# Linear attention and a Fourier feed-forward layer on one core: query loads split by row class and ordered by need, reciprocal roots taken per class, early k/v loads in another ring, and the first part of the program held in the planner's order

## Chip, cores, metric

One NeuronCore of a Trainium2 chip runs the whole program. The metric is the device time of one execution in microseconds; for the kernel before it is the median of three executions. The profile is one further, profiled execution.

## What is computed

For each of 8 batches, with 8 heads, 576 tokens and 64 channels per head:

```python
kv  = einsum('bhsd,bhse->bhde', k, v)
out = einsum('bhsd,bhde->bhse', q, kv)
x   = out / sqrt(mean(out * out, -1) + 1e-6) * g_norm      # then [batch, 576, 512]
X   = real(fft(fft(x, axis=1), axis=2))
u   = x + X
un  = (u - mean(u)) / sqrt(var(u) + 1e-6)
y   = u + maximum(un @ w_ch1, 0) @ w_ch2                   # 512 -> 2048 -> 512
```

Everything is float32; the weights come in as 64-bit floats.

## The kernel before

The work has two phases. Phase 1 goes batch by batch through attention, normalisation and the Fourier transform, and fills TensorE's gaps with a part of the feed-forward layer. Phase 2 is the rest of the feed-forward layer, block by block of 512 tokens.

One batch in phase 1 runs through these steps, in the names of the code:

- `plan_kv`: SyncE's queue loads k and v in four pairs of heads (`km`, `vm`, 256 KB each, from a ring `kv` of six buffers, L460) and a remainder (`kr`, `vr`, L469). For batch 0 the v loads go through ScalarE's queue. TensorE multiplies them into `ps_k` (L481).
- `plan_q_load` and `plan_q`: the queries come in two loads of 576 KB, one for each half of the tokens (`side`), at L504, and one more row of 2 KB (L510). The tokens of a half are dealt to three classes `j` (every third token). TensorE transposes each class (`ps_q`, L529), ScalarE copies it to `fq` (L533).
- `plan_out`: one output class `t` needs one query class of each side. TensorE writes two banks `ps_o` (L554); ScalarE copies (L569) and squares (L574) them, VectorE sums the squares (L578), GpSimd multiplies by `g_norm` (L589).
- `plan_y`: the reciprocal roots of all three classes at once: square root on ScalarE (L607), reciprocal on VectorE (L614), one refinement on GpSimd (L610, L618 to L620), the product on VectorE (L623).
- `plan_fold`: VectorE multiplies by the root (L651) and folds the halves (`ab`, L662), GpSimd adds and subtracts (`xe`, L669), ScalarE rounds to the high part `xh` (L675), GpSimd leaves the low part `xl` (L678).
- `plan_seq` (L693, L706, L710) and `plan_chn` (L727, L739, L747, L757): the Fourier transform along tokens and channels as matmuls with cosine and sine tables `cs` and `cd`, loaded and split once by `plan_dft` (L428, L431, L434).
- `plan_turn`: the result is transposed (L813) into blocks `unTh`, `unTl` of 512 tokens (L822, L825).

`plan_w` turns the feed-forward weights from 64-bit floats into two float32 parts: load (`raw`, 512 KB, L282), an Abs step on ScalarE (L285), five steps on VectorE (L292 to L302), a sum (L857), for the first matrix a mean (L307, L315) and its subtraction (L319), and the split (L861, L866). `plan_early` runs three of the sixteen slices of the feed-forward layer for a block (`ps_h` L354, `hh` L364, `hl` L367, `acc` L372) as soon as its tokens and the weights are there.

The order comes from a planner. Every step is an `op` with an engine, a cost in nanoseconds, a rank, the steps it follows and the ring buffers it takes; `Plan.run` walks through time, and on every free engine emits the ready step of lowest rank whose buffers are free. The ranks are 10 x batch + stage, and 1000 and more for the feed-forward filling. What it emits is then ordered once more by the Tile framework's scheduler, which may move an instruction past another on its engine. The rings are a fixed count of buffers per kind (`RINGS`); among them `h` has six buffers, used by `hh` and `hl`, and `part` two, used by the feed-forward partial sums.

## Time and profile before

| | us |
|---|---|
| median of 3 executions | 1024.72 |
| lowest, highest | 1024.54, 1029.22 |
| profiled execution | 1026.22 |
| its span | 1024.4 |
| TensorE busy | 993.9 (97%) |
| VectorE, ScalarE, GpSimd busy | 472.0, 322.4, 320.6 |

A view by windows gives, for each stretch of the span, the busy time and the number of instructions of TensorE, its weight loads (PEld), VectorE (DVE), ScalarE (ACT) and GpSimd (POOL), then TensorE's granted clock as a share of full speed, the mean busy share of the 16 DMA engines, and GB/s. Asked for one engine, it gives that engine's alone. In a timeline a row has its start, its length, engine, line, operation, output and inputs, and in brackets the idle time before it with what ended it; SPq is SyncE's queue issuing transfers, and the length of such a row is how long the queue was held. In the list of waits a row has who waited, for whom, total microseconds, times, and the longest. The chain of waits has start, length and what.

### The profile page before, as it was taken

The page shows a single profiled execution, that of the slowest core. Times are in us where ns is not written, and L with a number is a line of the kernel's source. Part 1 is how long each engine was busy: PE and PEld are TensorE (multiplying, and loading weights), DVE is VectorE, ACT ScalarE, POOL GpSimd, SP SyncE. Part 2 cuts the span into 40 slices and gives each one's busy share as a digit, 9 for nine tenths or more (in the row PEclk, how much of TensorE's full clock was granted, in tenths as well). Part 3 has the DMA queues.
Part 4 walks back from the last instruction along what each step waited for, and adds up shares of the span by engine and source line. Part 5 has one row for each costly group of instructions (what it writes and reads, how often), then busy time and mean ns, then how long its engine had stood idle before and what let it go on. Part 6 is the DMA issues. An engine that isn't in the chain of part 4 may idle for free.

```text
span 1024.4 us, 15026 instructions
## 1 busy us (share of the span) xinstructions
PE 993.9 (97%) x5866; PEld 839.4 (82%) x5866; DVE 472.0 (46%) x838; ACT 322.4 (31%) x655; POOL 320.6 (31%) x332
## 2 busy tenths in 40 slices
PE   4698999999999999999999999999999999999998
PEld 4697898889888888888888888888888888888886
DVE  4758775654588689998131314131221311311211
ACT  2456565555545434334221212021121021210110
POOL 0555876864865131225722303020020010110000
PEclk9998999999999999999999999999999999999999
DMA  9979979663246766645552515140320400400101
GB/s 245 253 164 280 190 214 263 168 182 139 88 162 212 275 206 253 228 136 175 155 177 74 182 51 170 71 139 1 125 81 0 165 21 1 164 1 1 42 1 41
DMA packets 109194, 140.70 MB, mean 137 GB/s; under 512 B 51790, under 2 KB 76418, under 8 KB 104516
## 3 DMA queue, kind: packets, MB, share of 16 engines
q1 hardware_dynamic: 105588, 132.28, 42.4%
q0 software_dynamic: 1920, 6.29, 2.0%
q10 hardware_dynamic: 1616, 1.18, 0.4%
q8 instruction: 46, 0.75, 0.3%
q14 instruction: 24, 0.20, 0.1%
HBM read 88.33 MB, written 51.40 MB: 136 GB/s over the span
## 4 chain that ended last, share of the span: by engine, by line
PE 93%; DMA 2%; DVE 2%; SPq 1%; issue 1%; ACT 0%; POOL 0%; DVEq 0%; ACTq 0%; POOLq 0%
PE ps_h L354 38%; PE acc L372 38%; PE ps_o L554 4%; PE ps_f L727 3%; PE ps_f L693 3%; PE ps_k L481 3%; PE ps_q L529 2%; PE ps_t L813 2%; DMA vm<-in_v_dram 2%; DVE x L651 1%; DMA qt<-in_q_dram 1%; SPq L510 1%; PE ps_w L315 0%; SPq L460 0%; DVE unTl L825 0%
## 5 line engine op out<-in xcount | busy, mean ns | idle before, releaser
L354 PE MATMUL ps_h<-unTh,w 128*128 128x512 f32 x1152 | 357.1, 391 | 0.0
L372 PE MATMUL acc<-w,hh 128*128 128x512 f32 x1152 | 345.0, 391 | 0.2 <-DVE unTl L825 0.2
L367 DVE SCALAR_TENSOR_TENSOR hl<-ps_h,hh 128x512 fp32r<-128x512 f32 x144 | 99.2, 689 | 379.8 <-ACT hh L364 377.5
L354 PEld LDWEIGHTS ps_h<-unTh,w 128*128 128x128 f32 x1152 | 215.4, 188 | 44.0
L372 PEld LDWEIGHTS acc<-w,hh 128*128 128x128 f32 x1152 | 214.9, 188 | 44.3 <-issue 0.3
L364 ACT ACTIVATE hh<-ps_h 128x512 fp32r<-128x512 f32 x144 | 85.9, 597 | 472.1 <-PE ps_h L354 442.9
L354 PE MATMUL ps_h<-unTl,w 128*128 128x512 f32 x576 | 224.5, 390 | 0.0
L372 PE MATMUL acc<-w,hl 128*128 128x512 f32 x576 | 213.1, 390 | 0.0
L354 PEld LDWEIGHTS ps_h<-unTl,w 128*128 128x128 f32 x576 | 108.3, 188 | 22.7
L372 PEld LDWEIGHTS acc<-w,hl 128*128 128x128 f32 x576 | 107.9, 188 | 22.5
L1133 POOL DMA_INDIRECT uu<-u_scr,rowidx x24 | 23.4, 974 | 286.2 <-DVE uu L1186 175.6
L589 POOL TENSOR_TENSOR x<-x,gb 96x512 f32<-96x512 f32 (+1 forms) x48 | 61.9, 1308 | 55.2 <-ACT x L569 40.6
L1152 POOL TENSOR_TENSOR uu<-uu,up 128x512 f32<-128x512 f32 x36 | 45.7, 1293 | 44.5 <-ACT up L1149 44.5
L554 PEld LDWEIGHTS ps_o<-kvt,fq 64*96 64x96 f32 (+1 forms) x768 | 42.7, 185 | 5.6 <-issue 3.2
L554 PE MATMUL ps_o<-kvt,fq 64*96 64x64 f32 (+1 forms) x768 | 47.0, 274 | 0.3 <-ACT fq L533 0.3
L481 PE MATMUL ps_k<-vm,km 128*64 128x64 f32 x512 | 28.7, 261 | 17.6 <-DMA vm<-in_v_dram 16.7
L1096 POOL TENSOR_TENSOR w<-wap,w 128x512 fp32r<-128x512 f32 x18 | 23.3, 1295 | 70.1 <-ACT w L1095 70.1
L1186 DVE SCALAR_TENSOR_TENSOR uu<-acc,rs_yb,uu 128x512 f32<-128x512 f32 x36 | 25.2, 745 | 42.5 <-PE acc L372 42.5
L578 DVE TENSOR_REDUCE ss<-ps_o 96x8 f32<-96x512 f32 (+1 forms) x48 | 32.2, 682 | 26.2 <-ACT ps_o L574 26.0
L669 POOL TENSOR_TENSOR xe<-ab 96x256 f32<-96x256 f32 (+1 forms) x48 | 37.5, 803 | 19.8 <-DVE ab L662 19.7
L693 PE MATMUL ps_f<-cs,xh 96*128 96x290 f32 (+1 forms) x192 | 41.8, 312 | 0.4 <-DVE x L651 0.4
L481 PEld LDWEIGHTS ps_k<-vm,km 128*64 128x64 f32 x512 | 22.9, 166 | 22.4 <-DMA km<-in_k_dram 16.2
(103 smaller groups left out, 1009.1 us busy)
## 6 DMA issues: line engine op xcount, KB each, us to landing
raw<-in_moe_w_ch_dram SPq DMA_DIRECT2D x32, 512.0 KB, 7.6
qt<-in_q_dram SPq DMA_DIRECT2D x16, 576.0 KB, 9.2
unT_scr<-unTh SPq DMA_DIRECT2D x9, 1024.0 KB
unT_scr<-unTl SPq DMA_DIRECT2D x9, 1024.0 KB, 6.3
part_scr<-part SPq DMA_DIRECT2D x36, 256.0 KB, 4.1
unTh<-unT_scr SPq DMA_DIRECT2D x9, 1024.0 KB, 4.9
unTl<-unT_scr SPq DMA_DIRECT2D x9, 1024.0 KB, 7.0
up<-part_scr SPq DMA_DIRECT2D x36, 256.0 KB, 3.0
```

Source lines behind the costliest of these rows:

```text
L354: nc.tensor.matmul(ps, w[c][:, kc * P : (kc + 1) * P], unT[a][:, kc, :], start=(idx == 0), stop=(idx == 3 * KC - 1),)
L364: nc.scalar.activation(hh, ps, AF.Relu)
L367: nc.vector.scalar_tensor_tensor(hl, ps, 0.0, hh.bitcast(F32), ALU.max, ALU.subtract)
L372: nc.tensor.matmul(acc, hpair[a][:, i * P : (i + 1) * P], w[c], start=(first and n == 0), stop=(last and n == 2),)
L481: nc.tensor.matmul(ps.t[s * D : (s + 1) * D, pr * D : (pr + 1) * D], km[:, s, j, :] if j < 4 else kr[:, h, :], vm[:, s, j, :] if j < 4 els ...
L554: nc.tensor.matmul(pss[s].t[:n, at : at + D], fqs[side].t[half, m, :n], kvt.t[half, m], start=True, stop=True,)
L578: nc.vector.tensor_reduce(ss.t[0][:n, :, t, s::2], pss[s].t[:n].rearrange("p (u m e) -> p u m e", u=2, e=D), AX.X, ALU.add,)
L589: nc.gpsimd.tensor_tensor(v_, v_, gb[:n].unsqueeze(1).to_broadcast([n, H, D]), ALU.mult)
L669: nc.gpsimd.tensor_tensor(o[:, s], a[:, 0], a[:, 1], ALU.subtract if s else ALU.add)
L693: nc.tensor.matmul(ps.t[:, :NS], xs[t].t[a][:n, part, ch * P : (ch + 1) * P], cs[:n, part, c, t, :], start=(idx == 0), stop=(idx == 8),)
L727: nc.tensor.matmul(ps.t[:n, :ND], pt.t[a][:, part, ch, offs[t] : offs[t] + n], cd[:, part, c, ch, :], start=(idx == 0), stop=(idx == 5),)
L1152: nc.gpsimd.tensor_tensor(us[j][i], us[j][i], part, ALU.add)
```

## The change

It has six parts.

- **Queries of batch 0 by class.** Each side's load becomes three loads of one class each (240 in the planner's size instead of 720), ranked by output class: side 0's class j by j/4, side 1's by (2-j)/4. A transpose follows its own class's load only.
- **Roots of batch 0 by class.** `plan_y` is called once per output class and works on a third of the columns; the temporaries `rs_s` and `rs_y` move into the ring `two`. The fold of a class follows its own root.
- **Rings.** The last pair of k and v of batch 0 and the last two of batch 1 take buffers of ring `h`; `ab` and `xe` of batch 0's third class take the two of ring `part`.
- **Weights.** The early weights' ranks become 4, 5, 6 (they were 4, 5, 6 as `rank(0, FOLD) + f` too), their loads' ranks 2, 4, 11 instead of 0, 3, 11.
- **Costs in the planner.** A pair of k and v counts 1080 instead of 520, an output class 1540 instead of 900, the copies of `plan_turn` more per column; TensorE's steps count twice until three steps of `plan_seq` have run.
- **The pin.** Each instruction that the planner emits up to 75,000 ns of its own time gets an order edge, without a semaphore, to the one emitted before it on its engine, so that the framework's scheduler keeps the planner's order there, on all five engines.

```diff
+EARLY_KV = (1, 2)
+W_CONV = (4, 5, 6)
+W_RANK = (2, 4, 11)
+PIN_UNTIL = 75000
...
+    def pin(self, emit, now):
+        tc = self.tc
+        traced = tc.nc.cur_bb.bb.instructions
+        start = len(traced)
+        emit()
+        traced = tc.nc.cur_bb.bb.instructions
+        for i in traced[start:]:
+            if i.engine not in self.pinned or now > PIN_UNTIL:
+                continue
+            last = self.last.get(i.engine)
+            if last:
+                tc.add_manual_dep(
+                    i, last,
+                    mybir.DependencyInfo(
+                        mybir.DependencyClass.NoSync, mybir.DependencyReason.DATA
+                    ),
+                    reason="the plan's order",
+                )
+            self.last[i.engine] = i.name
...
-                    o.emit()
-                    self.trace.append((t, t + o.cost, eng, o))
-                    end = free[eng] = t + o.cost
+                    self.pin(o.emit, t)
+                    cost = o.cost * (2 if eng == "PE" and cold > 0 else 1)
+                    cold -= o.dense
+                    self.trace.append((t, t + cost, eng, o))
+                    end = free[eng] = t + cost
...
-                main = Buf("kv", lambda c=c: qkv.tile([P, 2, 4, D], F32, name=c + "m", tag="m", bufs=RINGS["kv"]))
+                if b < 2 and pr >= NPAIR - EARLY_KV[b]:
+                    main = Buf("h", lambda c=c: base.tile(
+                        [P, 2, 4, D], F32, name=c + "m", tag="r", bufs=RINGS["h"]
+                    ))
+                else:
+                    main = Buf("kv", lambda c=c: qkv.tile(
+                        [P, 2, 4, D], F32, name=c + "m", tag="m", bufs=RINGS["kv"]
+                    ))
...
-            mm.append(op("PE", 520, rank(b, KV), go, ld + lds, [ps, kvt] + ts + rest))
+            mm.append(op("PE", 1080, rank(b, KV), go, ld + lds, [ps, kvt] + ts + rest))
...
+        if b == 0:
+            ld = [[dma(
+                240, rank(b, QT) + (2 - j if side else j) / 4,
+                lambda j=j: nc.sync.dma_start(
+                    qt.t[:TR, j].rearrange("p (h d) -> p h d", h=H), src[:, j]
+                ),
+                bufs=[qt],
+            )] for j in range(3)]
...
-        a = op("PE", 900, r, mm, done, [kvt, x, ss] + pss + fqs)
+        a = op("PE", 1540, r, mm, done, [kvt, x, ss] + pss + fqs)
...
+        n = TR + 1 if t is None else rows[t]
+        ts = slice(None) if t is None else slice(t, t + 1)
+        def of(a):
+            return a[:n].rearrange("p (s t h) -> p s t h", s=2, t=3)[:, :, ts]
...
-        ab, xe = e2_buf("ab"), e2_buf("xe")
+        if b == 0 and t == 2:
+            ab, xe = (Buf("part", part_tile) for _ in range(2))
+        else:
+            ab, xe = e2_buf("ab"), e2_buf("xe")
...
+        yp = bank_buf("ps_y")
+        if b == 0:
+            ys = [plan_y(b, ss, reds[t] + [one_row], yp, t) for t in range(3)]
+        else:
+            ys = [plan_y(b, ss, sum(reds, []), yp)] * 3
...
-                    plan_w(which, f, lambda: wA, rank(0, FOLD) + f, [], (0, 3, 11)[f])
+                    plan_w(which, f, lambda: wA, W_CONV[f], [], W_RANK[f])
```

The order of the instructions changes on every engine. Three places on two of them follow; the line numbers of the changed kernel are its own, some 40 to 60 higher.

On SyncE, at the start of the program, after the first k pair and its remainder, these transfers stand before (`raw` is a feed-forward weight, `gb` is `g_norm`, `qt` a query load):

```order
L460 DMA km<-in_k_dram 128x2x256 x2
L282 DMA raw<-in_moe_w_ch_dram 128x4x256
L460 DMA km<-in_k_dram 128x2x256
L282 DMA raw<-in_moe_w_ch_dram 128x1024
L412 DMA gb<-in_g_norm_dram 128x64
L504 DMA qt<-in_q_dram 96x24x64
L510 DMA qt<-in_q_dram 1x8x64
L504 DMA qt<-in_q_dram 96x24x64
```

And at the same place now:

```order
L507 DMA km<-in_k_dram 128x2x256 x3
L452 DMA gb<-in_g_norm_dram 128x64
L552 DMA qt<-in_q_dram 96x8x64
L566 DMA qt<-in_q_dram 1x8x64
L552 DMA qt<-in_q_dram 96x8x64 x5
L322 DMA raw<-in_moe_w_ch_dram 128x4x256
L322 DMA raw<-in_moe_w_ch_dram 128x1024
```

Batch 0's fourth k pair has moved up beside the others, the queries are six smaller loads, and both weights have moved behind them.

On SyncE, where batch 1's pairs are loaded, from the second pair on, before (`rowidx` is a table for phase 2):

```order
L460 DMA km<-in_k_dram 128x2x256
L460 DMA vm<-in_v_dram 128x2x256
L460 DMA km<-in_k_dram 128x2x256
L460 DMA vm<-in_v_dram 128x2x256
L413 DMA rowidx<-in_order_dram 128x36
L504 DMA qt<-in_q_dram 96x24x64
L510 DMA qt<-in_q_dram 1x8x64
L282 DMA raw<-in_moe_w_ch_dram 128x1024
L504 DMA qt<-in_q_dram 96x24x64
L460 DMA km<-in_k_dram 128x2x256
L460 DMA vm<-in_v_dram 128x2x256
```

And now:

```order
L507 DMA km<-in_k_dram 128x2x256
L507 DMA vm<-in_v_dram 128x2x256
L322 DMA raw<-in_moe_w_ch_dram 128x4x256
L507 DMA km<-in_k_dram 128x2x256
L507 DMA vm<-in_v_dram 128x2x256
L507 DMA km<-in_k_dram 128x2x256
L507 DMA vm<-in_v_dram 128x2x256
L560 DMA qt<-in_q_dram 96x24x64
L566 DMA qt<-in_q_dram 1x8x64
L560 DMA qt<-in_q_dram 96x24x64
```

The fourth pair has moved from behind batch 1's two query loads to ahead of them, and a weight load from inside the first pair to the place between the second and the third.

On TensorE, up to the first Fourier matmuls of batch 0 (the last row of each), before (`ps_w` is a weight's mean; `ps_o` is an output class of batch 1, sixteen instructions each, `ps_k` a pair of batch 2 here):

```order
L481 MATMUL ps_k<-vm,km 64x64 x8
L481 MATMUL ps_k<-vr,kr 64x64 x2
L315 MATMUL ps_w<-wp,mean_t 128x128
L481 MATMUL ps_k<-vm,km 64x64 x8
L481 MATMUL ps_k<-vr,kr 64x64 x2
L554 MATMUL ps_o<-kvt,fq 96x64 x16
L693 MATMUL ps_f<-cs,xh 128x290 x2
```

And now, with the transposes of batch 1's last queries (`ps_q`):

```order
L610 MATMUL ps_o<-kvt,fq 96x64 x16
L585 MATMUL ps_q<-ident,qt 128x96 x8
L528 MATMUL ps_k<-vm,km 64x64 x8
L528 MATMUL ps_k<-vr,kr 64x64 x2
L528 MATMUL ps_k<-vm,km 64x64 x8
L528 MATMUL ps_k<-vr,kr 64x64 x2
L752 MATMUL ps_f<-cs,xh 128x290 x2
```

Before, two output classes of batch 1 stand ahead of the Fourier matmuls (the first of them, in two halves, just above these rows); now one does, and the second stands behind them.

In the queues not shown: on ScalarE the first weight's Abs step now stands ahead of the copies of batch 0's first output class; on GpSimd one scaling by `g_norm` of batch 1 stands ahead of batch 0's last `xl`; on VectorE the three final products of batch 0's roots stand in a row behind the third class's reciprocal. Up to the third `hl`, VectorE has 127 instructions from the first weight step on before and 118 now, 63 of these behind the last low half of batch 0's first Fourier result.

More of the change, by code (lines that the diff above doesn't have):

```diff
@@ L37 @@
 PAD_RIGHT = 224
+EARLY_KV = (1, 2)
+W_CONV = (4, 5, 6)
+W_RANK = (2, 4, 11)
+PIN_UNTIL = 75000
+PINNED = {
+    mybir.EngineType.PE, mybir.EngineType.DVE, mybir.EngineType.Activation,
+    mybir.EngineType.Pool, mybir.EngineType.SP,
+}
 RINGS = {
@@ L67, with __init__ @@
     AHEAD = 4000
-    def __init__(self, rings):
+    def __init__(self, rings, tc=None):
+        self.tc, self.last = tc, {}
+        self.pinned = PINNED
         self.rings = dict(rings)
@@ L109, in run @@
         port = 0
+        cold = 3
         left = len(self.ops)
@@ L629, in plan_y @@
         c = op("POOL", 950, r, refine, [c, m], [ss])
-        return op("DVE", 200, r, last, [c], [ss, yp], port=True), yp
+        return op("DVE", 200, r, last, [c], [ss, yp], port=True)
     def plan_fold(b, t, x, y_done, yp, gs):
         n = rows[t]
-        ab, xe = e2_buf("ab"), e2_buf("xe")
+        if b == 0 and t == 2:
+            ab, xe = (Buf("part", part_tile) for _ in range(2))
+        else:
+            ab, xe = e2_buf("ab"), e2_buf("xe")
         xhl = Buf("xhl", lambda: [
@@ L651, in mul @@
                 nc.vector.tensor_tensor(v_, v_, y.unsqueeze(2).to_broadcast([n, H, D]), ALU.mult)
-            ms.append(op("DVE", 690, r, mul, [y_done, gs[s]], [x, yp]))
+            ms.append(op("DVE", 690, r, mul, [y_done] + gs[s], [x, yp]))
         def zero():
@@ L828, in low @@
                 )
-            h = op("ACT", 180 + 3 * (hi - lo), r, high, [a], [ps, unTs[j]])
-            turned[j] += [h, op("DVE", 180 + 4 * (hi - lo), r, low, [h], [ps, unTs[j]])]
+            h = op("ACT", 180 + 5.6 * (hi - lo), r, high, [a], [ps, unTs[j]])
+            turned[j] += [h, op("DVE", 180 + 5.3 * (hi - lo), r, low, [h], [ps, unTs[j]])]
     w_done = {}
@@ L939 @@
         ss = Buf("two", lambda: (
-            two.tile([P, 2, 3, H], F32, name="ss"), two.tile([P, 6 * H], F32, name="m")
+            two.tile([P, 2, 3, H], F32, name="ss"),
+            *[two.tile([P, 6 * H], F32, name=c) for c in ("m", "rs_s", "rs_y")],
         ))
@@ L949 @@
             for j in range(3):
-                fqs[side, 2 - j if side else j] = plan_q(b, side, j, qt, loaded)
+                fqs[side, 2 - j if side else j] = plan_q(b, side, j, qt, loaded[j])
         for t in range(3):
```

53 lines of the change are left out of this document (25 added, 28 removed).

## The prediction

> **What bounds the kernel now.** I read the page's header first, then the windows view cut where the profile changes, then the waits, then the timeline of SyncE's queue and of TensorE. The profiled execution took 1026.22 us around its span; the median of the three unprofiled runs is 1024.72, so I take differences on the trace and subtract them from the median. 0.5%, about what a measurement of this kernel can tell from no change, is 5.1 us.
>
> ```profile
> 0.00:60.60 60.60, 39.30 (x412) 34.30 (x412) 35.13 (x56) 24.93 (x50) 21.51 (x32) 1.00 1.09 238
> 60.60:66.00 5.40, 5.40 (x24) 5.37 (x23) 3.21 (x6) 3.26 (x7) 2.52 (x2) 1.00 0.66 221
> 88.90:92.00 3.10, 0.07 (x2) 0.04 (x2) 3.07 (x7) 3.10 (x7) 1.39 (x2) 0.71 0.96 302
> 92.00:97.00 5.00, 5.00 (x36) 4.47 (x37) 5.00 (x10) 2.54 (x7) 1.79 (x2) 0.50 0.97 341
> 97.00:125.00 28.00, 27.57 (x260) 23.51 (x260) 22.52 (x31) 15.19 (x35) 19.28 (x25) 1.00 0.96 217
> 125.00:1018.00 893.00, 892.57 (x4802) 750.29 (x4801) 384.28 (x697) 258.52 (x516) 258.78 (x254) 1.00 0.38 125
> ```
>
> The first number after each stretch's length is TensorE's busy time. From 125 us to the end nothing can be won by order: 892.57 of 893.00 us are matmul. What can be won lies before: 60.60 - 39.30 = 21.3 us of idle up to the first Fourier matmuls (L693), and 3.0 us at 88.9. There is a second loss in the busy time itself.
>
> ```profile
> 57.88 2.82 PE L554 MATMUL ps_o<-kvt,fq 64*96 64x64 f32 x32
> 84.32 1.57 PE L554 MATMUL ps_o<-kvt,fq 64*96 64x64 f32 x32
> ```
>
> The same 32 matmuls take 2.82 us at 58 us and 1.57 at 84: until 5.4 us into those Fourier matmuls TensorE runs at half rate, though the clock column of those windows says 1.00. So 39.3 + 5.4 = 44.7 us of early work contain about 22 us of excess, and the 5.00 us after the gap at 88.9 (clock 0.50) about 2.5. All losses together: 21.3 + 22 + 3.0 + 2.5 + 0.4, about 50 us; the change can only move these.
>
> What TensorE waits for there:
>
> ```profile
> PE ps_k L481 <- DMA vm<-in_v_dram: 16.7, 4, 8.3
> PE ps_q L529 <- DMA qt<-in_q_dram: 4.8, 2, 4.6
> SPq L460 <- PE ps_k L481: 21.7, 7, 9.4
> ```
>
> Loads of v and of queries; and SyncE's queue in turn waits 21.7 us (first 130 us) for TensorE to give back k and v buffers.
>
> **The change part by part.** *Queries by class, weights behind them.*
>
> ```profile
> 4.09 0.37 SPq L282 DMA_DIRECT2D raw<-in_moe_w_ch_dram  x1
> 7.54 0.34 SPq L282 DMA_DIRECT2D raw<-in_moe_w_ch_dram  x1
> 8.77 0.65 SPq L504 DMA_DIRECT2D qt<-in_q_dram  x1
> 9.47 5.18 SPq L510 DMA_DIRECT2D qt<-in_q_dram  x1
> 14.69 0.62 SPq L504 DMA_DIRECT2D qt<-in_q_dram  x1
> 21.80 0.90 PE L529 MATMUL ps_q<-ident,qt 96*128 96x96 f32 x4 [0.29 <-DMA qt<-in_q_dram]
> ```
>
> Two weight loads of 512 KB go ahead of the queries, whose last byte TensorE has at 21.80. Behind a query load the next issue is held 5.18 us, so splitting into classes moves the same pieces with 0.65 us more of issue for each of four extra loads: 2.6 us, or nothing where it falls into that hold; I take nothing, since the hold is longer. At the 238 GB/s of the first window the 1.05 MB of weights are 4.4 us: queries complete at 17.4.
>
> ```profile
> 22.63 1.55 PE L554 MATMUL ps_o<-kvt,fq 64*96 64x64 f32 x16
> 32.68 1.12 PE L481 MATMUL ps_k<-vm,km 128*64 128x64 f32 x16
> 11.79 0.62 ACT L285 ACTIVATE ps_a<-raw 128x512 f32<-128x512 f32 x1 [9.02 <-DMA raw<-in_moe_w_ch_dram]
> 12.44 0.70 DVE L292 TENSOR_SCALAR ps_a<-ps_a 128x512 f32<-128x512 f32 x1 [11.38 <-ACT ps_a L285]
> ```
>
> Before, batch 0's queries and outputs take TensorE from 21.80 to 32.68, 10.9 us. Now the first class (two groups of 1.55) is done while the last is loading, so 10.9 - 3.1 = 7.8 remain, to 25.2. On ScalarE the first weight's Abs step (L285 before) now stands ahead of that class's copies. Its weight lands half of 4.4 us behind the queries, at 19.6; some 1.5 us of this wait falls on the path: 26.7. The weights' work on VectorE starts 0.65 later, as 12.44 follows 11.79: near 20.3, 7.9 us later than before. That is the price of this edit, and it comes due below.
>
> *Buffers from the h ring.* Without them the fourth pairs of batches 0 and 1 wait for TensorE.
>
> ```profile
> 29.05 0.62 SPq L504 DMA_DIRECT2D qt<-in_q_dram  x1
> 35.48 4.74 SPq L460 DMA_DIRECT2D km<-in_k_dram  x1
> 40.27 4.99 DMA vm<-in_v_dram
> 45.39 1.12 PE L481 MATMUL ps_k<-vm,km 128*64 128x64 f32 x16 [8.27 <-DMA vm<-in_v_dram]
> 45.39 1.53 PE ps_k L481 x20
> 19.78 0.48 ACT L533 COPY fq<-ps_q 128x388 f32<-128x388 f32 x1 [4.26 <-PE ps_q L529]
> L578 DVE TENSOR_REDUCE ss<-ps_o 96x8 f32<-96x512 f32 (+1 forms) x48 | 32.2, 682 | 26.2 <-ACT ps_o L574 26.0
> L434 DVE TENSOR_TENSOR cs<-draw,cs 97x870 fp32r<-97x870 f32 x2 | 2.0, 1057 | 0.0
> ```
>
> Batch 1's fourth pair is queued behind two query loads and comes at 45.26. Now all four pairs are ahead of the queries, but a weight load stands between the second and the third, and waits until VectorE has read the first weight: five steps of 0.7 from 20.3, with two reductions (0.68 each) and one table half (1.06) between, 5.9 us: 26.2. The third pair then lands 5.0 us later (the 4.99 row), at 31.2, and TensorE is through with the fourth at 34.3, two pairs of 1.53 on. The query loads go out at about 29 (as before) and, one hold later, 34.5; the second lands 21.80 - 14.69 = 7.1 us after its issue, at 41.6. Then come four transposes (0.9), their copy (0.5), one output class (the 2.82 row), eight transposes (twice 0.9, less an overlap: 1.6), and two pairs of batch 2, 3.1 us, whose first loads follow the hold (34.5 + 5.2 + 5.0 = 44.7, in time). TensorE reaches the first Fourier matmuls at about 50.5; I take 50.
>
> *Roots by class, class 2 in the part ring.* The other side that these matmuls wait for is the last `xl`.
>
> ```profile
> 28.15 2.71 POOL L589 TENSOR_TENSOR x<-x,gb 96x512 f32<-96x512 f32 x2 [3.73 <-ACT x L569]
> 57.84 1.26 POOL L678 TENSOR_TENSOR xl<-xe,xh 96x512 fp32r<-96x512 f32 x1
> L569 ACT COPY x<-ps_o 96x512 f32<-96x512 f32 x6 | 3.3, 583 | 3.6 <-PE ps_o L554 3.6
> ```
>
> Before, it ends at 59.1, and TensorE still has outputs to do until 60.6. The class-wise roots are no shortcut here: on VectorE all three final products stand behind the third class's refinement. They add two more of each small step. Bounds: nothing for a third of the width each, or the whole width again: on VectorE 2 x (0.45 + 0.21) = 1.3 us.
>
> ```profile
> 38.32 0.45 DVE L614 RECIPROCAL rs_y<-rs_s 97x48 f32<-97x48 f32 x1
> 40.29 0.21 DVE L623 TENSOR_TENSOR ps_y<-rs_y,rs_s 97x48 f32<-97x48 f32 x1
> ```
>
> I take nothing, for batch 1's first scaling now stands ahead of the last `xl` on GpSimd anyway: it needs the output class that ends at 41.6 + 0.9 + 0.5 + 2.8 = 45.8, its two copies on ScalarE (0.58 each), then 1.36, half of the 2.71, and 1.26: 49.6. Both sides give 50. Were the class steps on the path, it would be 51.3.
>
> *The pin* adds no instruction. Its cost is that nothing can slip past a late head of a queue; the walk above pays it at the weight load on SyncE and at ScalarE's weight step.
>
> **The sum to the warm point.** One output class of batch 1 (2.8 us) is moved behind the first Fourier matmuls. Busy work ahead of it: 39.3 - 2.8 = 36.5; idle 50 - 36.5 = 13.5 against 21.3: 7.8 us won. Half-rate work falls from 44.7 to 41.9, excess from 22.35 to 20.95: 1.4 won. Together 9.2 us.
>
> **What comes due.** TensorE fills its gaps from 95.34 on with the feed-forward network, whose second half starts when VectorE has delivered three weights of each kind.
>
> ```profile
> 95.34 1.20 PE L354 MATMUL ps_h<-unTh,w 128*128 128x512 f32 x2
> 111.85 0.61 PE L372 MATMUL acc<-w,hh 128*128 128x512 f32 x2
> 60.71 7.55 PE ps_f L693 x36
> 12.40:111.85 99.45, 73.53 (x118) 0.97 1.01 225
> 70.00:111.85 41.85, 34.23 (x57) 0.92 1.00 239
> 106.28 3.12 DVE L662 TENSOR_TENSOR ab<-x 96x512 f32<-96x512 f32 x1
> ```
>
> The two windows are VectorE's alone. It worked 73.53 us on 118 recorded instructions, 0.62 us each, and was idle 25.9. In the new order 118 instructions stand up to the third `hl`, 63 of them behind the last low half of the Fourier result (L710 before). The Fourier matmuls end at 50 + 7.55 = 57.5; with a weight's mean and its subtraction ahead of that last half, about 0.7 each, it comes at 59. 63 x 0.62 = 39.3: without idle 98.3; at the 34.23 of 41.85 (82%) of before, 107. I take the middle, 102.7, as neither row is nearer. TensorE has then done 2.4 us less than before at 111.85 (one output class 1.57, and one pair, half of 1.53): ahead by 111.85 - 102.7 - 2.4 = 6.8 us; by the ends 11.2 and 2.5. Rounded to a gain of 7: 1024.72 - 7 = **1017.7 us**. That a VectorE instruction of 0.7 us can last 3.12 beside GpSimd is the reason not to take the good end.
>
> TensorE: Matmul & The Clock Gate in the Trainium skill (Part 1) states that about 3.4 us of sustained matmuls bring the full rate. The trace does not agree: before 60.6 TensorE was busy 15 us nearly without a break, and the 2.82 row is still half rate. By that rule the excess would have ended ahead of the Fourier matmuls in both kernels, and the sum to the warm point would be 7.8 instead of 9.2 us.
>
> **The rivals.** (1) *A wait cools TensorE again.* The gap of 3.03 us at 88.9 was followed by 5 us at clock 0.50. If VectorE's weights arrive in one late piece, TensorE stops 3 us or more between 60 and 105: 2.5 us more on top of the poor end, a gain of 0: 1024.7. For it: VectorE is 82% busy there; against it: outputs and transposes of batches 2 and 3 stand in between. The same page of the Trainium skill gives an idle window of about 3.4 us for this; the trace agrees, at 3.0. (2) *Loads bind.* If the weight load holds SyncE's queue not to 26.2 but to 30.6, everything behind it moves by 4.4 us and the gain shrinks to 2.6: 1022.1. For it: 21.7 us of such waits; against: its release is VectorE work that has no rival there. (3) *Weights late, slower than before.* VectorE starts the weights 7.9 us later and keeps the idle time of before, 25.9 us: 20.3 + 73.5 + 25.9 = 119.7, and TensorE, with its fillers used up, is behind by 119.7 + 2.4 - 111.85 = 10.3: 1035.0. For it: the later start; against it: much of the old idle time (TensorE's waits for the fourth pair) is what the buffers remove. It decides for slower by over 0.5% when VectorE's idle time from 20.3 on exceeds 20.8 us; my middle has 8.9. (4) *All hands over well*, VectorE at its good end and the gap at 88.9 gone: 11.2 + 3 = 14: 1010.7.
>
> **How the numbers follow.** Forecast (gain 2.5 to 11.2) 0.60, of which 0.08 lies below 5.1 us; rival 1 0.12, rival 2 0.10, rival 3 0.10, rival 4 0.08. Faster: 0.52 + 0.08 = 0.60; same: 0.08 + 0.12 + 0.10 = 0.30; slower 0.10. The range reaches from between rival 4 and the good end, 1010, to rival 1, 1024.5; rival 3 and half of rival 4 are left out.
>
> **What would show it.** Right: the first Fourier matmuls start near 50 (before 60.6), queries complete near 17.4, the feed-forward network's first matmul near 80 and second half near 103, the windows after 125 as full as before. Wrong: the first Fourier matmuls later than 55 (loads), a gap of over 3 us with half clock after it (rival 1), the second half later than 115 (rival 3), or idle time after 125.

## The result and the profile after

The changed kernel takes 1031.78 us (median of ten executions, 1029.36 to 1035.75) against 1026.73 for the kernel before beside it (1024.54 to 1029.22): a ratio of 1.0051, interval 1.0036 to 1.0065. It is slower by half a per cent, where 1017.7 was forecast. The profiled execution is the longest of the ten (1035.75), so its losses are some 4 us larger than the median's. Medians and ratios below leave out three executions more than 1.5% above the fastest of their kernel: 1649.9 us in run 3, 1043.9 in run 6 and 1351.9 of the kernel before.

The span and TensorE's busy time stand at the head of the page, before:

```profile
span 1024.4 us, 15026 instructions
...
PE 993.9 (97%) x5866; PEld 839.4 (82%) x5866; DVE 472.0 (46%) x838; ACT 322.4 (31%) x655; POOL 320.6 (31%) x332
```

and after:

```profile
span 1034.0 us, 15035 instructions
...
PE 1003.9 (97%) x5866; PEld 846.5 (82%) x5866; DVE 473.3 (46%) x842; ACT 322.5 (31%) x657; POOL 325.0 (31%) x340
```

TensorE's idle time (span less busy) is 30.5 us before and 30.1 after. The same 5866 matmuls are busy 10.0 us longer, so in sum the 9.6 us by which the span grew are work at a lower rate. The equal idle time is a sum of two changes: 6.4 us less up to the first Fourier matmuls, 6.0 more behind them. The windows of after, cut where the profile changes, show where (after the length: TensorE's busy time first, the granted clock third from the end):

```profile
0.00:50.50 50.50, 35.61 (x378) 30.97 (x378) 28.55 (x47) 24.73 (x50) 22.87 (x40) 1.00 1.04 247
50.50:56.00 5.50, 5.50 (x24) 5.48 (x23) 5.24 (x9) 0.82 (x2) 1.23 (x1) 1.00 1.13 224
...
71.80:74.80 3.00, 0.06 (x4) 0.04 (x2) 3.00 (x9) 2.00 (x7) 2.84 (x5) 0.75 1.08 284
74.80:97.50 22.70, 22.53 (x198) 18.58 (x198) 11.17 (x21) 7.62 (x18) 6.10 (x10) 0.58 1.01 278
...
101.30:105.20 3.90, 0.03 (x2) 0.01 (x1) 3.90 (x7) 1.32 (x3) 3.27 (x5) 0.85 0.66 134
105.20:111.00 5.80, 5.80 (x33) 4.96 (x34) 5.73 (x9) 2.95 (x7) 4.30 (x7) 0.51 0.09 15
...
182.40:190.00 7.60, 7.60 (x54) 5.76 (x54) 4.87 (x8) 3.40 (x8) 2.51 (x2) 0.55 1.26 261
190.00:1018.00 828.00, 827.49 (x4211) 694.51 (x4209) 348.46 (x629) 224.57 (x437) 218.46 (x207) 1.00 0.36 118
```

Up to the first Fourier matmuls 14.9 us are idle (50.50 - 35.61; before 21.3). At about 56 us, in these matmuls, TensorE reaches full rate (two of them take 0.69 us at 55.04 and 0.43 at 56.39): the warm point. Then come three gaps (the third, of 1.5 us, ends at 182.4), each followed by a stretch at about half rate: 22.53 x (1 - 0.58) = 9.5 us lost from 74.8 on, 5.80 x 0.49 = 2.8 from 105.2, 7.60 x 0.45 = 3.4 from 182.4. That is an estimated 15.7 us lost to half rate behind the warm point, against the 2.5 of before. From 190 us on TensorE is as full as before.

The gaps and the milestones in TensorE's timeline of after:

```profile
50.52 0.85 PE L752 MATMUL ps_f<-cs,xh 97*128 97x290 f32 x2
...
71.16 0.69 PE L528 MATMUL ps_k<-vm,km 128*64 128x64 f32 x16
74.79 0.48 PE L528 MATMUL ps_k<-vr,kr 64*64 64x64 f32 x4 [2.94 <-DMA vr<-in_v_dram]
...
105.19 0.80 PE L394 MATMUL ps_h<-unTh,w 128*128 128x512 f32 x1 [3.87 <-ACT w L921]
...
115.31 0.73 PE L412 MATMUL acc<-w,hh 128*128 128x512 f32 x2
```

The first Fourier matmuls start at 50.52 (before 60.6). But batch 3's first pair of k and v runs its 16 main matmuls at 71.16 and then stands before its remainder (`kr`, `vr`) until 74.79, with nothing else to do in between. The second half of the feed-forward network starts at 115.31 (before 111.85). SyncE's timeline, with the remainder's two loads and what stands ahead of them:

```profile
64.89 0.34 SPq L322 DMA_DIRECT2D raw<-in_moe_w_ch_dram  x1
66.54 0.37 SPq L507 DMA_DIRECT2D km<-in_k_dram  x1
66.96 0.46 SPq L507 DMA_DIRECT2D vm<-in_v_dram  x1
67.68 0.65 SPq L516 DMA_DIRECT2D kr<-in_k_dram  x1
68.39 0.62 SPq L516 DMA_DIRECT2D vr<-in_v_dram  x1
```

The queue's longest wait between 50 and 78 us, for VectorE to have read the buffer of an earlier weight:

```profile
SPq L322 <- DVE wp L342: 8.6, 1, 8.6
```

The sixth weight's load held SyncE's queue for 8.6 us, to 64.9, and `vr` was used 6.4 us after its issue.

### The profile page after: what moved, and what is told of

Same layout as the page of the kernel before. It is cut to its first block, busy times and chain, and to the rows that moved or that the text cites. A ratio compares the mean times of both kernels' runs of the same rounds, so it can differ in the third digit from the quotient of the medians.

```text
span 1034.0 us, 15035 instructions
## 1 busy us (share of the span) xinstructions
PE 1003.9 (97%) x5866; PEld 846.5 (82%) x5866; DVE 473.3 (46%) x842; ACT 322.5 (31%) x657; POOL 325.0 (31%) x340
## 4 chain that ended last, share of the span: by engine, by line
PE 90%; DMA 4%; DVE 2%; SPq 1%; issue 1%; ACT 1%; DVEq 0%; ACTq 0%
PE ps_h L394 37%; PE acc L412 37%; PE ps_f L752 4%; PE ps_f L787 3%; PE ps_o L610 3%; PE ps_k L528 2%; PE ps_t L873 2%; PE ps_q L585 1%; DMA vr<-in_v_dram 1%; DMA draw<-in_dft_s_dram 1%; DMA part_scr<-part 1%; DMA qt<-in_q_dram 1%; DMA vm<-in_v_dram 1%; SPq L566 0%; DVE ab L721 0%
## 5 line engine op out<-in xcount | busy, mean ns | idle before, releaser
L610 PEld LDWEIGHTS ps_o<-kvt,fq 64*96 64x96 f32 (+1 forms) x768 | 45.0, 191 | 6.3 <-issue 4.2
L610 PE MATMUL ps_o<-kvt,fq 64*96 64x64 f32 (+1 forms) x768 | 49.4, 280 | 0.0
L1205 DVE BATCH_NORM_STATS2 bst<-uu 128x6 f32<-128x512 f32 x36 | 24.5, 688 | 27.3 <-DMA uu<-u_scr,rowidx 18.7
```

Source lines behind the costliest of these rows:

```text
L610: nc.tensor.matmul(pss[s].t[:n, at : at + D], fqs[side].t[half, m, :n], kvt.t[half, m], start=True, stop=True,)
```

## The experiments

All were timed beside the kernel before, which stood at 1025.5 to 1027.0 in each group; "extra" is work that computes nothing. Span, busy and idle are those of one profiled execution of each, in us (idle is span less busy; without the extra work the matmuls are the same 5866, and busy times differ by the rate). The number of the run stands in front:

```
    kernel                                      span  busy    idle  median  ratio (interval)
    before                                    1024.4   993.9  30.5
    changed                                   1034.0  1003.9  30.1  1031.8  1.0051 (1.0036-1.0065)
 1  + 24 dense extra at 71 us                 1023.9   996.4  27.5  1026.6  1.0009 (0.9994-1.0024)
 2  + remainder's own buffers                 1029.5  1002.4  27.1  1031.5  1.0049 (1.0034-1.0063)
 3  without pin                               1036.2  1004.8  31.4  1037.5  1.0084 (1.0055-1.0113)
 4  before + pin                              1024.3   997.8  26.5  1026.2  1.0008 (0.9995-1.0020)
 5  dense extra, third weights early          1035.6  1006.6  29.0  1034.5  1.0083 (1.0059-1.0107)
 6  third weights early                       1033.5  1007.4  26.1  1032.9  1.0067 (1.0045-1.0090)
 7  + 24 small extra at 71 us                 1026.8   998.3  28.5  1030.2  1.0034 (1.0019-1.0049)
 8  + 24 dense extra at 71 and 24 at 100      1027.5  1000.5  27.0  1030.6  1.0049 (1.0030-1.0067)
 9  + dense extra at 71, 92 and 170           1025.9  1000.2  25.7  1027.7  1.0006 (0.9992-1.0021)
10  before + 24 dense extra at 87             1028.3   999.2  29.1  1029.4  1.0031 (1.0017-1.0044)
11  old planner costs                         1027.9   996.5  31.4  1030.3  1.0039 (1.0021-1.0057)
12  no buffers from the h ring                1030.4  1001.8  28.6  1032.2  1.0053 (1.0034-1.0072)
13  sixth weight's load later                 1016.8   990.7  26.1  1018.5  0.9934 (0.9918-0.9950)
16  the same, once more                       1016.8   993.2  23.6  1019.0  0.9923 (0.9905-0.9942)
15  its order, load where it was              1018.7   991.2  27.5  1022.0  0.9972 (0.9946-0.9998)
14  load later + remainder's own buffers      1025.3   997.2  28.1  1027.5  1.0014 (0.9996-1.0031)
```

The theory was that the wait at 71.8 us takes TensorE's clock away, and that this, not the waiting, is the loss; the rival, that TensorE is late because its operands are, whatever its clock.

**1. Keep the clock through the wait.**

```
+ if b == 3 and pr == 0:
+     for _ in range(24):
+         nc.tensor.matmul(ps.t[:, 256:512], cs[:TR, 0, 0, 0, :P], cs[:TR, 0, 0, 0, :256], start=True, stop=True)
```

> The changed kernel with 24 matmuls of 128x256 more, into an unused half of a bank, ahead of batch 3's first k/v pair, where TensorE waited 2.94 us from 71.8; their results are not used. Theory (clock): that wait lets TensorE fall to half rate, and the small matmuls behind it do not bring it back until 97.5. With dense work in the gap the 22.5 us behind it run at full rate: 9 to 14 us less than the changed kernel's 1031.8, so 1018 to 1023, although there is more work. Rival (weights late): TensorE is held by VectorE's late third weight either way; it only waits longer at 101: 1029 to 1034.

Measured 1026.6, level with the kernel before: 3.1 us more work, about 5 us less time. The extra matmuls in the timeline, and behind them the pair and its remainder at full rate, without a wait:

```profile
70.76 3.12 PE L527 MATMUL ps_k<-cs 96*128 96x256 f32 x24
73.81 0.69 PE L534 MATMUL ps_k<-vm,km 128*64 128x64 f32 x16
```

The windows of the same run:

```profile
56.00:89.70 33.70, 32.78 (x427) 29.02 (x425) 27.75 (x53) 21.26 (x50) 18.73 (x21) 1.00 0.84 256
89.70:93.40 3.70, 0.10 (x2) 0.05 (x1) 3.70 (x3) 2.29 (x7) 3.07 (x4) 0.90 1.11 302
93.40:99.00 5.60, 5.60 (x15) 4.38 (x16) 4.84 (x8) 0.75 (x2) 2.87 (x5) 0.50 0.77 155
```

Full rate to 89.7, then a second gap, 3.6 us behind VectorE, and 5.6 us at half rate. The order is that of the changed kernel up to about 77 us; from there outputs and transposes interleave a little differently. The theory holds for the first gap, but the time missed its 1018 to 1023: with the clock kept TensorE still waits, and cools, at the second gap.

**2. The remainder in buffers of its own** (so that its load need not wait for batch 2's).

```
+ if b == 3: kr = Buf("h", ...)   # for k and for v
```

> The changed kernel with batch 3's k and v remainder in two buffers of ring h, so that their loads need not wait for batch 2's last pair. Theory (clock): the 2.94 us wait goes without any filler, and the half-rate stretch with it: 1017 to 1023. Rival (weights late): no gain, 1029 to 1034.

Measured 1031.5, a miss. The wait for the remainder went, the next pair's `vm` came 1.2 us late, and that was enough. The windows around it:

```profile
70.00:71.00 1.00, 0.10 (x4) 0.00 (x0) 0.48 (x2) 1.00 (x3) 1.00 (x2) 1.00 1.04 340
71.00:72.00 1.00, 0.70 (x14) 0.66 (x15) 0.76 (x2) 0.45 (x2) 1.00 (x2) 1.00 1.08 364
72.00:73.00 1.00, 1.00 (x10) 0.72 (x8) 0.29 (x1) 0.61 (x2) 0.93 (x1) 0.96 1.02 292
73.00:74.00 1.00, 1.00 (x9) 0.72 (x8) 0.87 (x3) 0.81 (x4) 0.91 (x2) 0.50 1.19 288
```

TensorE stops at 70.1, works again from 71.3 at full rate, and loses the clock at 72.9, in the middle of work.

**3 and 4. The pin.** The changed kernel without it, and the kernel before with it.

```
- PIN_UNTIL = 75000
+ PIN_UNTIL = -1
```

> The changed kernel without the pin, all else kept. Theory (clock): what counts is whether a wait near 3 us falls behind the warm point; the remainder's load waits as before, so about the same, 1028 to 1034, unless the free order puts dense work there. Rival (the pin holds instructions behind late heads of queues): 1022 to 1027.

> The kernel before with the pin alone, 75 us of the planner's time. Theory (clock): no query or weight load is moved, so the first Fourier matmuls stay near 60; 1023 to 1031 by where the waits fall. Rival (the pin is the harm): 1031 or more.

Measured 1037.5 and 1026.2. The pin is not the cost: without it the changed kernel is no faster (its first Fourier matmuls start at 54.58), and the time of the kernel before stays. Run 4's profile shows something else, though. It loses the clock at 82.6 us:

```profile
82.00:96.70 14.70, 14.02 (x114) 12.65 (x115) 11.90 (x24) 9.14 (x20) 6.82 (x10) 0.54 0.93 273
```

That is 14.02 x 0.46 = 6.4 us lost, 3.9 more than in the kernel before, in the same time, as the wait of 3.0 us at 88.9 is gone and TensorE is idle 4.0 us less. Half rate cost nothing there: it stood in the place of waiting.

**5 and 6. The third weights earlier**, with and without the extra matmuls of run 1, for the wait of 3.9 us at 105 us.

```
- W_CONV = (4, 5, 6)
- W_RANK = (2, 4, 11)
+ W_CONV = (4, 4, 5)
+ W_RANK = (2, 3, 5)
```

> The changed kernel with the 24 extra dense matmuls ahead of batch 3's first k and v pair, and the third weights of the feed-forward network ranked earlier (conversion ranks 4, 4, 5 in place of 4, 5, 6, load ranks 2, 3, 5 in place of 2, 4, 11), so that VectorE makes the third first-matrix weight some 20 instructions earlier. Theory (two causes that add up: the cooling behind the waited-for remainder, and the third weight that comes late and cools TensorE a second time): against the kernel with the extra matmuls alone (1026.6) the wait of 3.6 us and the half-rate stretch behind it, about 2.8 us, go: 1019 to 1022. Rival (VectorE as a whole is late, and a weight moved ahead only makes the low halves late instead): the wait moves to the first second-half matmul and the time stays at 1025 to 1029.

> The changed kernel with the third weights ranked earlier alone (conversion ranks 4, 4, 5, load ranks 2, 3, 5), without extra matmuls. Theory of two causes: the cooling at 75 us stays (about 10 us of half-rate excess up to 97 us), the wait of 3.9 us and the half rate behind it (2.8) go: 1024 to 1027, with a granted clock of about half from 75 us on. Rival (everything hangs on the first cooling; the late weight is only what half rate made of it, and would be late again): 1029 to 1033.

Measured 1034.5 and 1032.9: run 5 slower than either theory had it, run 6 at the end of its rival's range, but not by the rival's way. The wait for the weight is gone in both, but VectorE does this work ahead of the turned blocks and sums, and loads wait for TensorE further on. In the run with extra matmuls:

```profile
185.64 1.12 PE L534 MATMUL ps_k<-vm,km 128*64 128x64 f32 x16 [3.76 <-DMA vm<-in_v_dram]
```

In this trial the late third weight could not be moved away by itself: VectorE's work has to stand somewhere.

**7. Small extra matmuls in place of dense ones** (64 rows by 64 columns of the array).

```
- ps.t[:, 256:512], cs[:TR, 0, 0, 0, :P], cs[:TR, 0, 0, 0, :256]
+ ps.t[:D, 256:512], cs[:D, 0, 0, 0, :D], cs[:D, 0, 0, 0, :256]
```

> The changed kernel with the 24 extra matmuls ahead of batch 3's first k and v pair again, as many columns long, but on 64 rows by 64 columns of the array and not 97 by 128: the same number of instructions and the same stream, a third of the array at work. Theory a (what keeps the clock is the work of the array, not that an instruction runs): the clock falls at about 75 us as without them, 1029 to 1033. Theory b (any busy TensorE keeps it, the idle time alone cools): full rate up to 90 us, 1025 to 1028, as with the dense ones.

Measured 1030.2, by time theory a. The windows say otherwise:

```profile
71.20:83.50 12.30, 10.37 (x144) 8.87 (x142) 10.66 (x21) 6.80 (x18) 8.07 (x12) 1.00 0.94 245
83.50:90.00 6.50, 6.07 (x52) 5.00 (x53) 0.84 (x2) 0.72 (x2) 0.00 (x0) 0.74 0.97 320
```

The small matmuls held the full rate up to 83.5. It fell behind a later wait for `vm` (2.4 us at 81.6), which in run 1's profile isn't there. Two of the twelve executions took 1024.9 and 1025.1, ten 1028.1 to 1030.6. So theory b on the clock in this stretch: 24 small matmuls kept it as 24 dense ones did. Run 16 shows below that small matmuls do not always keep it.

**8, 9 and 10. More extra matmuls, and extra matmuls in the kernel before.** Run 8 adds 24 ahead of the third weight's matmuls; run 9 has 24 behind batch 3's last pair and 12 ahead of batch 6's first; run 10 puts 24 into the gap that the kernel before has at 88.9.

```
  8: + if f == 2 and j == 0: 24 of them, ahead of ffn1
  9: + if b == 3 and pr == NPAIR - 1: fill(24)   + if b == 6 and pr == 0: fill(12)
 10: + if b == 3 and pr == 3: 24 of them, in the kernel before
```

> The changed kernel with the 24 extra dense matmuls ahead of batch 3's first k and v pair, and 24 more of the same ahead of the first matmuls that use the third first-matrix weight, where TensorE waits 3.6 us for it. The weight comes no sooner, but TensorE should not be at half rate behind it. Theory (the half rate behind a wait is a price of its own): 2.5 to 3 us off the 1026.6 of the single fill, 1023 to 1024.5, and no wait shown there. Rival (the half rate there is hidden by what VectorE has still to do): 1026 to 1027.5, unchanged.

> The changed kernel with extra dense matmuls (128x256, 0.13 us each at full rate) at three places where TensorE waits or is about to: 24 ahead of batch 3's first k and v pair as before, 24 behind batch 3's last pair (ahead of the 3.6 us wait for VectorE at 90 us), 12 ahead of batch 6's first pair (ahead of a wait of 1.5 us at 172 us). They compute nothing. Theory (waits in themselves cost little more than their length; half rate behind them is what the change lost): no half rate after 56 us, and against the 1026.6 of the single fill the 2.8 us behind the wait at 93 us and 1.5 us behind that at 173 us go: 1021 to 1024, below both kernels. Rival (TensorE cannot use the rate, because what it waits for, VectorE and the loads, comes no sooner): 1026 to 1029; and with the fills in the wrong place they cost their own 4.7 us: 1031.

> The kernel before with 24 extra dense matmuls ahead of batch 3's last k and v pair, for which it waits 3.0 us at 89 us and then runs 5 us at clock 0.54. They compute nothing. The order behind them moves a little. Theory (a cooling costs what runs at half rate before the next dense stretch): about 2.5 us of half rate go, 1023 to 1025. Rival (in the kernel before that stretch has slack): 1026 to 1028. If it gains as much as the same fill in the changed kernel (5 us, to 1021.5), the change did not make cooling dearer.

Measured 1030.6, 1027.7 and 1029.4, three misses. Run 8 put them behind the 3.6 us wait instead of into it, and took 4.0 us longer than run 1 for 3.1 us more work; its profile also loses the clock at 82 us, behind a wait of 1.2 us for `vm` that run 1 does not have. Run 9 saved the clock at 97 us but met another late `vm` at 83.4 and the old one at 174. In run 10 the gap was filled and the clock kept; then another load came late:

```profile
87.21 3.14 PE L480 MATMUL ps_k<-cs 96*128 96x256 f32 x24
90.88 0.69 PE L487 MATMUL ps_k<-vm,km 128*64 128x64 f32 x16 [0.53 <-DMA vm<-in_v_dram]
...
104.61 0.33 PE L487 MATMUL ps_k<-vr,kr 64*64 64x64 f32 x4 [1.85 <-DMA vr<-in_v_dram]
```

with half rate behind it to about 115. Filling a wait did not repair what makes loads late.

**11 and 12. Parts of the change undone:** the planner's costs (`cold`, pairs, output classes, turned blocks), and the buffers from the h ring.

```
 11: 1080 -> 520, 1540 -> 900, 5.6 -> 3, 5.3 -> 4, cold = 3 -> 0
 12: EARLY_KV = (1, 2) -> (0, 0)
```

> The changed kernel with the planner's costs of the kernel before (pair of k and v 520 and not 1080, output class 900 and not 1540, the two halves of a turned block 3 and 4 per row and not 5.6 and 5.3, no doubled cost up to the third dense step). Classes of queries, buffers from the h ring, weights' ranks and the pin stay. It puts batch 2's first two pairs behind the first Fourier matmuls. Theory a (the new costs make the order in which batch 3's loads come late): the wait at 72 us is gone and the time is 1022 to 1027. Theory b (loads and VectorE are late in any order of this kind): a wait of over 1 us between 62 and 95 us with half rate behind it, 1029 to 1035.

> The changed kernel without the buffers from the h ring for the last pairs of batches 0 and 1 (all k and v tiles from their own ring, as before). Theory (the buffers bring the earlier first Fourier matmuls, and the cooling at 72 us comes in any case): first Fourier matmuls 3 us or more later than 50.5 us, and 1033 to 1037. Rival (the buffers only shift load, and what comes earlier is lost behind): 1029 to 1033, no different from the changed kernel.

Measured 1030.3 and 1032.2. With the old costs TensorE runs at half rate from about 80 us on, behind four waits of 0.45 to 0.94 us between 71 and 79 us: theory b in its effect, though no single wait reaches 1 us there. Without the early buffers the first Fourier matmuls start hardly later:

```profile
51.39 0.85 PE L752 MATMUL ps_f<-cs,xh 97*128 97x290 f32 x2
```

0.9 us against the 3 expected: the rival. The buffers bring 0.9 us of the 10 by which these matmuls moved, not more.

**13 and 14. The sixth weight's load behind batch 3's first loads**, alone, and with the remainder's own buffers.

```
+ if (which, f) == (2, 2): w_late[:] = [a]               # plan_w: its load
+ if b == 3 and pr in (0,): w_late[0].after += ld + lds   # plan_kv (14: both of the first pairs)
- self.pin(o.emit, t)
+ self.pin(o.emit, 0 if o in w_late else t)
```

> The changed kernel with one load moved on SyncE's queue: the sixth weight (second matrix, third part), which in the changed kernel stands ahead of two pairs and the remainder of k and v and holds the queue from 56.2 to 64.9 us until VectorE has read the buffer, now stands behind batch 3's first loads, pinned there. Nothing else is changed by hand; the order behind 75 us of the plan moves a little. Theory a (the wait of 2.9 us at 71.8, and so the cooling, comes from that held queue): no wait above 0.5 us between 66 and 78 us, full rate up to 85 us or longer, and 1022 to 1027 without any extra work. Theory b (the remainder's own buffers, which come free only when batch 2's last pair is done, hold it): a wait of 1 to 3 us at about 72 us stays, half rate behind it, 1029 to 1033.

> As in the run before, the sixth weight's load behind batch 3's first two pairs, and batch 3's remainder of k and v in buffers of the h ring, so that it need not wait for batch 2's. The remainder in the h ring alone gave 1031.5 and a wait of 1.2 us on the next pair, whose load stood behind the weight's. Theory a (the held queue is the cause): no wait above 0.5 us from 56 to 80 us, the clock stays, 1021 to 1026. Theory b (with the loads on time VectorE is late all the same: the wait moves to the first matrix's matmuls at 90 to 105 us, and TensorE cools there): 1026 to 1031.

Run 13 took 1018.5 (1018.04 to 1019.31): faster than the kernel before by 0.66%, and by the ratios some 12 us below the changed one. Its TensorE timeline at the same place, and the first second-half matmul:

```profile
70.75 0.69 PE L534 MATMUL ps_k<-vm,km 128*64 128x64 f32 x16
71.37 0.88 PE L879 MATMUL ps_t<-ident,x 96*128 96x96 f32 x8
72.18 0.38 PE L616 MATMUL ps_o<-kvt,fq 64*96 64x64 f32 x2
73.20 0.33 PE L534 MATMUL ps_k<-vr,kr 64*64 64x64 f32 x4 [0.65 <-DMA vr<-in_v_dram]
...
104.28 0.73 PE L415 MATMUL acc<-w,hh 128*128 128x512 f32 x2
```

Its windows:

```profile
73.20:85.20 12.00, 11.92 (x184) 10.63 (x184) 11.93 (x23) 7.85 (x19) 9.34 (x13) 1.00 1.01 295
85.20:87.30 2.10, 0.01 (x3) 0.01 (x1) 2.10 (x5) 2.10 (x6) 1.08 (x1) 1.00 1.17 230
87.30:90.80 3.50, 3.50 (x9) 2.73 (x10) 3.50 (x7) 1.85 (x5) 3.50 (x3) 0.54 1.08 310
```

The wait is 0.65 us and the clock stays; one gap of 2.1 us remains, with 1.6 us of half rate behind it (3.50 x 0.46). But theory a was wrong on the way there. Its SyncE queue is held just as long, now by k and v buffers that TensorE gives back:

```profile
SPq L510 <- PE ps_k L534: 9.5, 1, 9.5
```

and issues the remainder no sooner:

```profile
68.92 0.63 SPq L519 DMA_DIRECT2D vr<-in_v_dram  x1
...
76.37 1.12 SPq L325 DMA_DIRECT2D raw<-in_moe_w_ch_dram  x1
```

`vr` is used 4.3 us after its issue and not 6.4. The weight's 512 KB are no longer ahead of it, but in run 15, where they are, it is 4.8, so they alone do not make the difference. And the order that the planner made along with this puts eight transposes and two output matmuls ahead of the remainder. Run 14 took 1027.5: another order, a wait for `vm` of 1.9 us at 82 us, and half rate behind it.

**15 and 16. The order or the load?** Run 13's order on TensorE (but for one pair behind 104 us), VectorE, ScalarE and GpSimd, with the sixth weight's load back in its old place; and run 13 once more beside it.

```
- self.pin(o.emit, 0 if o in w_late else t)
+ self.pin(o.emit, t)
```

> The same order on TensorE, VectorE, ScalarE and GpSimd as in the run that moved the sixth weight's load (1018.5), but for one pair of batch 4 behind 104 us; on SyncE that load alone stands where the changed kernel has it, ahead of batch 3's first loads. Theory a (the load itself, its hold on the queue and its 512 KB ahead of the remainder, is the cause): the remainder arrives 2 us later again, a wait of over 2 us at about 72 us with half rate behind it, 1026 to 1033. Theory b (the order on TensorE, which puts eight transposes and the first outputs ahead of the remainder, and the first matrix's matmuls later, is the cause): no wait above 1 us, 1017 to 1021, with the load where it was.

> The run with the sixth weight's load moved once more, beside the one with the load put back, on one chip. If the gain is the kernel's and not that chip's, 1017 to 1021 again, below the kernel before by 0.4% or more; else near the kernel before, 1024 to 1028.

Measured 1022.0 and 1019.0. With the load in its old place SyncE and TensorE show:

```profile
64.72 0.34 SPq L325 DMA_DIRECT2D raw<-in_moe_w_ch_dram  x1
...
68.21 0.62 SPq L519 DMA_DIRECT2D vr<-in_v_dram  x1
```

```profile
72.98 0.33 PE L534 MATMUL ps_k<-vr,kr 64*64 64x64 f32 x4 [1.13 <-DMA vr<-in_v_dram]
```

Here 1.13 us of wait did not cost the clock in the profiled execution, nor did 1.23 us at 86.1; it fell at 96, behind a wait of 3.0 us for ScalarE. Of its twelve executions eight took 1018.7 to 1023.3 us and four 1028.0 to 1032.1. Seven of the twelve ran at a mean clock of 0.990 or less; of the eleven of runs 13 and 16, with the load moved, none (0.994 or more, 1016.5 to 1020.7 us). So by the ratios the order gives about 8 of the 12 us, and the load's place shifts how often TensorE loses the clock. Which part of the order it is, the transposes ahead of the remainder or what stands behind, was not tried apart, and where the four longest executions lost the clock their times alone don't show.

Run 16's profiled execution (1018.65 us) shows two more things. From 64 us on it has no wait longer than 0.3 us, at the remainder too, and yet the clock falls at 79.6, in the middle of outputs:

```profile
72.17 0.33 PE L534 MATMUL ps_k<-vr,kr 64*64 64x64 f32 x4 [0.23 <-DMA vr<-in_v_dram]
```

```profile
79.00:80.00 1.00, 1.00 (x16) 1.00 (x15) 1.00 (x2) 0.57 (x2) 0.69 (x2) 0.81 1.00 333
80.00:81.00 1.00, 1.00 (x12) 1.00 (x12) 1.00 (x4) 0.72 (x2) 0.00 (x0) 0.50 0.98 349
```

Half rate lasts to 89.9, some 5.1 us of lost work, and still it took no longer than run 13's profiled execution (1018.57), which instead waits 2.1 us for VectorE at 85.2 and loses 1.6 to half rate behind that. So no long wait was needed for the clock to fall, and half rate was a loss only as far as TensorE would not have waited anyway.

## Why the prediction was wrong

- *The walk to the warm point* was right, and in its path: the query loads go out at 29.26 and 35.03 (29 and 34.5), the last `xl` ends at 50.50 (49.6). One step was luckily harmless: batch 1's fourth pair is done at 38.4 and not 34.3, which the later queries hide. First Fourier matmuls at 50.52 (50 forecast); idle ahead of them 14.9 us against 21.3, 6.4 won (7.8); half-rate work up to 56 us 35.61 + 5.50 = 41.1, its excess 1.8 less than before (1.4). 8.2 us in all, 9.2 forecast.
- *Buffers from the h ring*: the step gave them the fourth pairs; they are worth 0.9 us (run 12). The gain is that of the other parts. Which of these brings it was not tried.
- *What comes due*: 102.7 for the first second-half matmul, measured 115.31. With the wait at 72 us out of the way (runs 13 and 16) it starts at 104.28 and 103.7, and the kernel takes 1018.5 and 1019.0, where 1017.7 was forecast. But these have another order. In run 1, which keeps the clock to 89.7 in nearly the changed kernel's, it starts at 106.99, the term's poor end (107). So the middle is not shown for the order that was forecast. In the changed kernel VectorE's sums and the third weight stood behind a single instruction, and TensorE's wait at 105 us behind these:

```profile
97.83 4.09 DVE L721 TENSOR_TENSOR ab<-x 97x512 f32<-97x512 f32 x1
```

- *The step that failed* is the one from the warm point to the time: the sum carries 6.8 us of lead to the end and has no term for what TensorE waits and loses to half rate behind the warm point. Measured in the profiled executions, it waits 6.0 us more there and loses some 13.2 more to half rate (15.7 against 2.5), against 8.2 won ahead. Together that is 11.0 us, where the span grew by 9.6; the losses to half rate are estimates from the granted clock.
- *Rival 1, a wait cools TensorE again*, had the mechanism and gave it 0.12, with "2.5 us more on top of the poor end". That price was read from before, where dense matmuls came 3.4 us behind the gap (95.34 against 91.99) and ended the half rate. In the changed kernel the gap at 71.8 is followed by transposes, pairs and outputs; half rate lasted to 93.8, and cost 9.5 us of work, not 2.5, and 6.2 more behind two further gaps. Run 1 shows what the first cooling is worth in time: with the wait filled the changed kernel is level with before, 5 us faster in spite of 3.1 us more work. What keeps run 1 from the forecast is not taken apart; the wait of 3.6 us for VectorE and the half rate behind it are in it.
- The reason given against rival 1, that outputs and transposes of batches 2 and 3 stand in between, does not hold for the wait at 71.8: none stand between batch 3's first pair and its remainder. Where some do (runs 13 and 15), most of the loss is gone.
- *Rival 2* put its hold at the weight load of 26.2 us. The weight load that mattered was a later one, at 64.9, and less than the order on the engines: with that load in its place run 15 keeps about 8 of the 12 us. *Rival 3* (slower, VectorE late) had the sign and not the cause: run 1 takes away the loss against the kernel before without touching VectorE's work.
- Where the prediction let a window of idle time of about 3.4 us (the Trainium skill, "TensorE: Matmul & The Clock Gate", Part 1) agree with the gap of 3.0 us, the traces disagree. The clock fell 1.3 us into that very gap:

```profile
90.00:91.00 1.00, 0.00 (x0) 0.00 (x0) 1.00 (x3) 1.00 (x3) 0.00 (x0) 0.61 0.93 329
```

An idle stretch of 1.2 us was followed by half rate in run 2, and in run 16 no wait was longer than 0.3. So short waits behind the warm point, for which the sum has no term, could go with a long stretch at half rate.

## What to carry over

Price a wait on TensorE by the work that would follow it at half rate up to the next dense stretch, not by its length: here 2.9 us of waiting went with 9.5 us of lost work. Then take off what TensorE would have waited for other engines anyway, as runs 4 and 16 show. When a change brings work forward, read the new order at every load that TensorE needs directly behind another, and ask what it can do in between if that load is 2 us late. Where the executions of a kernel lie in two groups, as run 15's do, look for a stretch in which the clock sometimes falls.

## What the hardware showed that was not expected

- The length of a gap did not decide whether the clock fell. It fell behind idle stretches of 1.20 us (run 2, 2.8 us after the gap began and 1.6 us into full-rate work) and 1.23 us (run 8), and in run 16 without one above 0.3 us; it did not behind 1.13 and 1.23 us in run 15, nor behind 0.65 in run 13. What does decide is not shown.
- Small matmuls kept the full rate in one place (run 7: 24 of 64x64 did as well as 24 of 96x128) and lost it in another (run 16, after 15 us of pairs, transposes and outputs). In the changed kernel 13.5 us of almost nothing else, from 74.8 on, did not bring it back; the 128x512 matmuls from 88.3 on did, 5.5 us later:

```profile
93.00:94.00 1.00, 1.00 (x11) 1.00 (x13) 0.36 (x1) 0.60 (x1) 0.00 (x0) 0.60 0.99 393
```

- The VectorE instruction of 4.09 us stood beside four of GpSimd that took 5.47 us (95.90 to 101.37); the same operation on the next block, at 102.45, took 0.83, though GpSimd was at work then as well (102.00 to 105.23). What stretched the first is not shown.
